# Seven on-chip slots instead of one for the first phase's g blocks

## The chip, the cores and the metric

The kernel runs on one core of a Trainium2 chip. The metric is the device time of one execution in microseconds (us). The kernel before takes 461.11 us, the median of three runs (458.97 to 461.44).

## The reference

Three layers run one after the other on 2304 tokens (4 batches of 576) of width 512. Only what bears on the change is given in full:

```python
def reference(q, k, v, w_in, w_out, phi, w1, w2):
    x = attention(q, k, v)                        # [2304, 512]; local heads and strided heads
    h = x @ w_in                                  # [2304, 2048]
    g = h * (1.0 / (1.0 + np.exp(-1.702 * h)))
    x = g @ w_out                                 # [2304, 512]
    logits = x @ phi                              # [2304, 32]
    d = softmax(logits, axis=0)                   # over tokens
    c = softmax(logits, axis=1)                   # over the 32 slots
    slot_input = d.T @ x                          # 8 experts, 4 slots each
    slot_out = [relu(s @ w1[e]) @ w2[e] for e, s in enumerate(slot_input)]
    return c @ slot_out
```

## The kernel before

**Tiling.** The tokens are cut into six chunks (`LIVE`): four steps of up to 512 tokens, then 256 each. The 2048 columns of g are cut into 16 blocks f of 128. A step is a pair (c, f): chunk c outer, block f inner, 96 steps in all. The first phase is c = 0, the second c = 1, and so on.

**One step** (`moe_step`, L374). `gemm1` (L326) makes h for the step: 12 matmuls of 128x128 by 128x512 into one of two PSUM tiles (`ps_h`, two buffers, L334). Then ScalarE writes tanh(0.851 h) into an SBUF slot (L339) and VectorE turns this in place into (tanh + 1) * h (L340). That is twice g. A slot is a 128x512 piece of the tile `gT` (19 of them), picked by `g_slot` (L310).

**What happens to g.** In c = 0 the logits can't be formed yet, because the second weight matrix is not converted. So each block is written to DRAM (`g_scr`, L398) from the SP queue, and the slot is given back at once in the program's order (L399). From c = 3 on, pieces of it are read back (L324). In c = 1 and later, g stays on chip: VectorE transposes it into the slot numbered f of `gT` (L362), and four blocks at a time go into the logits (`lg`, L354). The first `lg` matmuls come in the middle of c = 1, after the step (1, 4).

**Which slot.** `g_slot` takes the first free one of slots 16 to 18 (with `NF` = 16), then 14 and 15. Since L399 frees the slot in every step of c = 0, all 16 blocks of that phase get slot 16. The tile framework adds the wait that this needs: the tanh of block f+1 may write only when the transfer of block f out of the slot has landed.

**What else runs in these phases.** The weights come as 64-bit numbers (`wraw`) and are converted on chip. `load_w` (L262) needs one ScalarE operation (L268), one on GpSimd (L269) and three on VectorE (L270, L271, L272). For the first weight matrix follow a rounded copy on ScalarE (L279) and the remainder on GpSimd (L280). The raw input of the first matrix lies in slots 0 to 11 of `gT` (L255 to L259), in pairs used in turn by six blocks. In c = 0, the 16 blocks of the first matrix are converted two to three steps ahead, and then the second matrix's, which are written to `wo_scr` (L284), transposed (L287) and multiplied by phi (L297, L303). Between these steps a generator runs the attention of the next batch: scores `s` (L167), mask, maximum and exp (L170, L180, L185), normalising on GpSimd (L188), transposes `ptp` (L203), products `av` (L222) and copies into x (L247, L248).

**What sets the order.** Each engine executes its own queue in order, and so does SP with its DMAs. The order in these queues is not that of the source: a scheduler in the tile framework orders the instructions by its own estimates of when each could start, and the slot of g is one of the things that it sees.

Of the kernel before, what the change touches and what calls it, by code (L numbers as in the profile page):

```python
# [33 lines left out]
NF = FF // 128  # L34
# [10 lines left out]
def tile_kernel(ctx: ExitStack, tc: tile.TileContext, lqk, lv, sqk, sv, wraw, phi, wexp, cst, out):  # L45
# [207 lines left out]
    def load_raw(f, k):  # L253
        if gt and k == 0:
            r = 2 * (f % 6)  # L255
            raw = gt[0][:, r:r + 2].rearrange("p a b -> p (a b)").bitcast(U32).rearrange("p (a b) -> p a b", b=2)
        else:
            raw = rawp.tile([P, 512, 2], U32, tag="raw", name=f"raw_{f}_{k}")
        nc.sync.dma_start(raw.rearrange("p a b -> p (a b)"), wraw[f, k].bitcast(U32))  # L259
        raws[f, k] = raw  # L260

    def load_w(f, k):  # L262
        if (f, k) not in raws:
            load_raw(f, k)
        raw = raws.pop((f, k))
        t = rawp.tile([P, 512], F32, tag="wc", name=f"wc_{f}_{k}", bufs=4)
        u = t.bitcast(U32)
        nc.scalar.activation(t, raw[:, :, 1].bitcast(F32), AF.Abs)  # L268
        nc.gpsimd.tensor_scalar(t, t, F64_LARGE, F64_SMALL, op0=ALU.min, op1=ALU.max)  # L269
        nc.vector.tensor_scalar(u, u, 3, 0x3FFFFFF8, op0=ALU.logical_shift_left, op1=ALU.bitwise_and)  # L270
        nc.vector.scalar_tensor_tensor(u, raw[:, :, 1], 0xC0000000, u, op0=ALU.bitwise_and, op1=ALU.bitwise_or)  # L271
        nc.vector.scalar_tensor_tensor(u, raw[:, :, 0], 29, u, op0=ALU.logical_shift_right, op1=ALU.bitwise_or)  # L272
        conv[f, k] = t

    def split(f):
        if f % 2 == 0:
            wis[f // 2] = wip.tile([P, 2, 2, 512], F32R, tag="wi", name=f"wi_{f // 2}")
        w, t = wis[f // 2][:, f % 2], conv.pop((f, 0))
        nc.scalar.copy(w[:, 0], t)  # L279
        nc.gpsimd.tensor_tensor(w[:, 1], t, w[:, 0].bitcast(F32), op=ALU.subtract)  # L280

    def wo_transpose(f):
        t = conv.pop((f, 1))
        nc.sync.dma_start(wo_scr[f], t)  # L284
        tp = mtile(f"wot_{f}")
        for kt in range(4):
            nc.tensor.transpose(tp[:, 128 * kt:128 * kt + 128], t[:, 128 * kt:128 * kt + 128], ident)  # L287
        woT[f] = rawp.tile([P, 4, 128], F32, tag="woT", name=f"woT_{f}", bufs=1)
        nc.scalar.copy(woT[f].rearrange("p k f -> p (k f)"), tp)
# [3 lines left out]
    def wo_phi(f):  # L293
        t = woT.pop(f)
        pw = mtile(f"wp_{f}")[:, :P]
        for kt in range(4):
            nc.tensor.matmul(pw[32 * kt:32 * kt + 32], phs[:, kt, :], t[:, kt, :], start=True, stop=True)  # L297
        wpT[f] = rawp.tile([P, P], F32, tag="wpT", name=f"wpT_{f}", bufs=2)
        nc.scalar.mul(wpT[f], pw, 0.5)

    def wo_phi_sum(f):
        pw = mtile(f"wq_{f}")[:, :NS]
        nc.tensor.matmul(pw, wpT.pop(f), sel, start=True, stop=True)  # L303
        nc.scalar.copy(wp[:, f, :], pw)
# [3 lines left out]
    slots, taken, where = {}, set(), {}  # L308

    def g_slot(c, f):  # L310
        k = next(k for k in [*range(NF, NF + 6), NF - 2, NF - 1] if k in slots and k not in taken)
        assert k >= NF or c < 2
        taken.add(k)
        where[c, f] = k
        return slots[k]
# [5 lines left out]
    def g_open(c, f):  # L321
        g = gs[c, f] = g_slot(c, f)
        if c in KEPT:
            nc.scalar.dma_start(g[:, :256], g_scr[f, :, KEPT[c]:KEPT[c] + 256])  # L324

    def gemm1(c, f):  # L326
        c0, N = LIVE[c]
        x, w = xt[c0 // 512], wis[f // 2][:, f % 2]
        xs = slice(c0 % 512, c0 % 512 + N)
        h = ps_h.tile([P, 512], F32, tag="h", name=f"h_{c}_{f}")  # L330
        n = 0
        for kt in range(4):
            for we, xe in ((0, 0), (0, 1), (1, 0)):
                nc.tensor.matmul(h[:, :N], w[:, we, 128 * kt:128 * kt + 128], x[xe][:, kt, xs], start=n == 0, stop=n == 11)  # L334
                n += 1
        if (c, f) not in gs:
            g_open(c, f)
        g = gs[c, f][:, 256:] if c in KEPT else gs[c, f][:, :N]
        nc.scalar.activation(g, h[:, :N], AF.Tanh, scale=0.851)  # L339
        nc.vector.scalar_tensor_tensor(g, g, 1.0, h[:, :N], op0=ALU.add, op1=ALU.mult)  # L340
# [8 lines left out]
    def logits(c, f0):  # L349
        N = WIDTH[c]  # L350
        if f0 == 0:
            lgs[c] = ps_lg.tile([P, 512], F32, tag="lg", name=f"lg_{c}")
        for j in range(4):
            nc.tensor.matmul(lgs[c][32 * j:32 * j + 32, :N], wp[:, f0 + j, :], gs[c, f0 + j][:, :N], start=f0 == 0, stop=f0 == NF - 4)  # L354
            g_used(c, f0 + j)

    def g_transpose(c, f):
        N = WIDTH[c]
        if c < 5:
            assert f not in taken  # L360
            taken.add(f)
        nc.vector.transpose(t_slots(c)[:, f, :N], gs[c, f][:, :N])  # L362
        g_used(c, f)
# [4 lines left out]
    def moe_step(i):  # L368
        c, f = steps[i]
        j = i - NF  # L370
        for n in (i + 4, i + 5):
            if n < NF and (n, 0) not in raws and n not in done_in:
                load_raw(n, 0)
        if i + 3 < NF:  # L374
            done_in.add(i + 3)
            load_w(i + 3, 0)
        if 0 <= j + 3 < NF:
            load_w(j + 3, 1)
        if 0 <= j < NF:
            wo_phi(j)  # L380
        if 0 < j < NF:
            wo_phi_sum(j - 1)
        for s in list(side):
            if next(s, True):
                side.remove(s)
        if i + 2 < NF:
            split(i + 2)
        if c == 1 or f >= TFROM:
            for _ in range(1 if c == 1 else 2):
                if todo and (c > 1 or todo[0][1] not in taken):  # L390
                    g_transpose(*todo.pop(0))
        while todo and todo[0][0] < c and todo[0][1] not in taken:
            g_transpose(*todo.pop(0))
        gemm1(c, f)
        if 0 <= j + 1 < NF:
            wo_transpose(j + 1)
        if c == 0:
            nc.sync.dma_start(g_scr[f], gs[c, f])  # L398
            taken.discard(where.pop((c, f)))  # L399
            return  # L400
        if j and f % 4 == 0:
            pc, pf = steps[i - 4]
            logits(pc, pf)
            if f == 0:
                side.append(post(pc))
        todo.append((c, f))
        if f + 1 < NF and c in KEPT:
            g_open(c, f + 1)
# [172 lines left out]
    for i, (c, f) in enumerate(steps):  # L581
        if f == 0 and c < 3:
            side.append(attention_steps(c + 1))
            next(side[-1])
        if (c, f) == (2, 0):
            wo_phi_sum(NF - 1)
            raw_es.close()
            accp = acc_es.enter_context(tc.tile_pool(name="accp", bufs=1))
            sp_["p"] = accp
            acc = accp.tile([P, 4, 512], F32, name="acc")  # L590
            more = accp.tile([P, 3, 512], F32, name="more")
            slots.update({NF + 3 + k: more[:, k] for k in range(3)})
        if (c, f) == (3, 2):
            att_es.close()
            e1p = ctx.enter_context(tc.tile_pool(name="e1p", bufs=4, side="right"))
            for _ in range(4):
                load_ex(e1p, "e")
            for e in (1, 0, 1):
                load_ex(xp, f"x{e}")
        if (c, f) == (5, 1):  # L600
            for e in range(2):
                load_ex(xp, f"x{e}")
        moe_step(i)
        if (c, f) == (5, 4):
            for k in range(2):
                load_ex(None, gx_tile())
        if c == 5 and f % 2:
            load_ex(wip, "wi")
# [4 lines left out]
    c = len(LIVE) - 1  # L613
# [231 lines left out]
```

## Time and profile before

| | |
|---|---|
| median of three runs | 461.11 us |
| the profiled execution | 463.21 us |
| its span in the trace | 461.1 us |
| TensorE (PE) busy | 418.4 us, 91% |
| VectorE (DVE) busy | 272.1 us, 59% |
| ScalarE (ACT) busy | 197.2 us, 43% |
| GpSimd (POOL) busy | 77.8 us, 17% |
| DRAM written | 13.11 MB |

The span goes from the first instruction to the last; 2.1 us of the profiled execution lie outside it. These shares are means over stages that have different limits, so the sections below look at stretches of the span. Times in the trace are us from its start. A TensorE block `h` is 12 matmuls. Busy PE means that a matmul is under way, whatever the clock that was granted to it; that clock is given as a fraction of full speed.

### The profile page before, as it was taken

To read this page: it belongs to the slowest core of one execution; us is meant where nothing else is said; L and a number is where in the kernel's file an instruction comes from. 1 tells how busy PE (TensorE), PEld (TensorE's weight loads), DVE (VectorE), ACT (ScalarE), POOL (GpSimd) and SP (SyncE) were. 2 spreads that over 40 slices of the span, in tenths; PEclk is the share of its full clock that TensorE was granted. 3 is DMA by queue.
4 is the path that set the end of the run, shared out by engine and by line. 5 is a ranking of instruction groups with operands and counts; after the bars stand their busy time and mean duration, and the time that the engine had idled before them with its cause. 6 is when DMAs were issued, how large, how long until landed. Compare 5 with 4: busy or idle time off the path is not lost.

```text
span 461.1 us, 10584 instructions
## 1 busy us (share of the span) xinstructions
PE 418.4 (91%) x4272; PEld 302.4 (66%) x4277; DVE 272.1 (59%) x580; ACT 197.2 (43%) x656; POOL 77.8 (17%) x96
## 2 busy tenths in 40 slices
PE   8969859578979999999999999999999999799964
PEld 4746647456757777777767767778778797244654
DVE  2784999992737667755564565477486464432212
ACT  3876567653645566755634353212212222120311
POOL 0461658830121111100210010000000000010000
PEclk9999978799989999999999999999999999899985
DMA  8966766267643747125020016922122998879996
GB/s 234 374 180 248 217 218 230 73 209 267 173 148 92 230 136 221 72 91 179 18 93 22 16 42 215 383 69 70 48 59 70 353 354 316 342 280 427 422 347 208
DMA packets 32528, 89.32 MB, mean 194 GB/s; under 512 B 2912, under 2 KB 14304, under 8 KB 28384
## 3 DMA queue, kind: packets, MB, share of 16 engines
q1 hardware_dynamic: 27872, 84.45, 52.7%
q10 hardware_dynamic: 4608, 4.20, 3.0%
q8 instruction: 34, 0.56, 0.5%
q14 instruction: 14, 0.11, 0.1%
HBM read 75.53 MB, written 13.11 MB: 192 GB/s over the span
## 4 chain that ended last, share of the span: by engine, by line
PE 67%; DVE 16%; DMA 7%; ACT 4%; issue 2%; POOL 2%; SPq 0%; ACTq 0%; POOLq 0%
PE h L334 37%; PE u L462 4%; PE lg L354 4%; DMA out<-gT 4%; DVE wc L271 4%; PE s L167 4%; DVE wc L272 3%; PE hp L677 3%; PE av L222 2%; PE op L707 2%; PE ptp L203 2%; DVE wc L270 2%; ACT ts L185 2%; DMA qk<-lqk 2%; PE wot L287 1%
## 5 line engine op out<-in xcount | busy, mean ns | idle before, releaser
L334 PE MATMUL h<-x,wi 128*128 128x512 f32 (+1 forms) x1152 | 231.1, 353 | 15.7 <-DVE gT L340 15.3
L334 PEld LDWEIGHTS h<-x,wi 128*128 128x128 f32 x1152 | 179.7, 195 | 57.9 <-issue 17.2
L340 DVE SCALAR_TENSOR_TENSOR gT<-gT,h 128x512 f32<-128x512 f32 (+1 forms) x78 | 44.3, 568 | 66.0 <-ACT gT L339 65.2
L339 ACT ACTIVATE gT<-h 128x512 f32<-128x512 f32 (+1 forms) x78 | 39.1, 501 | 76.0 <-PE h L334 65.2
L185 ACT ACTIVATE ts<-ts,nmx 128x64 f32<-128x64 f32 (+1 forms) x120 | 41.6, 350 | 27.0 <-DVE nmx L180 27.0
L188 POOL TENSOR_TENSOR ts<-ts,sm 128x384 f32<-128x384 f32 (+2 forms) x32 | 28.6, 894 | 132.5 <-DVE sm L187 75.1
L362 DVE STREAM_TRANSPOSE gT<-gT 128x512 f32<-128x512 f32 (+1 forms) x62 | 40.0, 651 | 3.1 <-DMA gT<-g_scr 1.6
L269 POOL TENSOR_SCALAR wc<-wc 128x512 f32<-128x512 f32 x32 | 23.5, 739 | 51.7 <-ACT wc L268 48.6
L203 PE MATMUL ptp<-cs,ts 128*96 128x128 f32 (+1 forms) x120 | 18.7, 290 | 10.0 <-POOL ts L188 8.5
L167 PE MATMUL s<-qk 64*64 64x96 f32 (+1 forms) x552 | 26.3, 236 | 0.3 <-DMA qk<-lqk 0.3
L167 PEld LDWEIGHTS s<-qk 64*64 64x64 f32 x552 | 21.5, 134 | 6.4 <-issue 4.5
L270 DVE TENSOR_SCALAR wc<-wc 128x512 uint32<-128x512 uint32 x32 | 19.4, 617 | 10.4 <-POOL wc L269 8.5
L280 POOL TENSOR_TENSOR wi<-wc,wi 128x512 fp32r<-128x512 f32 x16 | 22.9, 1439 | 8.7 <-ACT wi L279 6.4
L203 PEld LDWEIGHTS ptp<-cs,ts 128*96 128x96 f32 (+1 forms) x120 | 13.8, 141 | 16.0 <-POOL ts L188 13.8
L735 POOL MEMSET hz<- 128x512 f32 x4 | 2.1, 560 | 126.9 <-PE spp L630 126.9
L248 DVE TENSOR_TENSOR x<-av,x 128x320 fp32r<-128x320 f32 (+20 forms) x54 | 19.5, 393 | 6.0 <-ACT x L247 5.6
L185 ACT ACTIVATION_READ_ACCUMULATOR ts<-ts,nmx 128x1 f32 x120 | 22.8, 190 | 0.0
L247 ACT CAST x<-av 128x320 fp32r<-128x320 f32 (+20 forms) x54 | 19.0, 397 | 8.8 <-PE av L222 4.6
L462 PE MATMUL u<-gT,dT 32*32 32x512 f32 x576 | 20.9, 615 | 1.9 <-DVE z L437 1.9
L339 ACT ACTIVATE more<-h 128x256 f32<-128x256 f32 (+1 forms) x18 | 7.7, 427 | 34.5 <-PE h L334 28.1
L186 DVE TENSOR_SCALAR sm<-sm 128x5 f32<-128x5 f32 (+2 forms) x32 | 7.9, 247 | 22.7 <-ACT ts L185 22.7
L354 PE MATMUL lg<-gT,wp 128*32 128x512 f32 (+1 forms) x124 | 21.1, 563 | 0.0
(127 smaller groups left out, 509.7 us busy)
## 6 DMA issues: line engine op xcount, KB each, us to landing
ex<-wexp SPq DMA_DIRECT2D x28, 1024.0 KB, 8.2
raw<-wraw SPq DMA_DIRECT2D x19, 512.0 KB, 4.8
gT<-wraw SPq DMA_DIRECT2D x13, 512.0 KB, 4.4
qk<-lqk SPq DMA_DIRECT2D x8, 592.0 KB, 5.8
g_scr<-gT SPq DMA_DIRECT2D x16, 256.0 KB, 3.0
wo_scr<-wc SPq DMA_DIRECT2D x16, 256.0 KB, 2.3
ex<-wo_scr SPq DMA_DIRECT2D x4, 1024.0 KB, 9.2
gT<-wexp SPq DMA_DIRECT2D x4, 1024.0 KB, 7.0
```

Source lines behind the costliest of these rows:

```text
L167: nc.tensor.matmul(sp[hs, u], t[hs, qo:qo + 64], t[hs, ko + qo:ko + qo + nk], start=not early, stop=not early or u == nt - 1)
L185: nc.scalar.activation(ts[:, u], src[:, u], AF.Exp, scale=sc, bias=nmx[:, u:u + 1], accum_out=sm[:, u:u + 1])
L188: nc.gpsimd.tensor_tensor(ts, ts, sm[:, :nt].unsqueeze(2).to_broadcast([P, nt, nk]), op=ALU.mult)
L203: nc.tensor.transpose(ptp[:nk, u - a], src, ident)
L269: nc.gpsimd.tensor_scalar(t, t, F64_LARGE, F64_SMALL, op0=ALU.min, op1=ALU.max)
L270: nc.vector.tensor_scalar(u, u, 3, 0x3FFFFFF8, op0=ALU.logical_shift_left, op1=ALU.bitwise_and)
L334: nc.tensor.matmul(h[:, :N], w[:, we, 128 * kt:128 * kt + 128], x[xe][:, kt, xs], start=n == 0, stop=n == 11)
L339: nc.scalar.activation(g, h[:, :N], AF.Tanh, scale=0.851)
L340: nc.vector.scalar_tensor_tensor(g, g, 1.0, h[:, :N], op0=ALU.add, op1=ALU.mult)
L354: nc.tensor.matmul(lgs[c][32 * j:32 * j + 32, :N], wp[:, f0 + j, :], gs[c, f0 + j][:, :N], start=f0 == 0, stop=f0 == NF - 4)
L362: nc.vector.transpose(t_slots(c)[:, f, :N], gs[c, f][:, :N])
L462: nc.tensor.matmul(us[a][32 * j:32 * j + 32, :].rearrange("p (t f) -> p t f", f=32), dT[q, 32 * b:32 * b + 32], gT[q, :, 32 * b:32 * b + 3 ...
```

## The change

In c = 0, block f takes slot 12 + f % 7, so that slots 12 to 18 are used in turn. None of them is one of the slots 0 to 11 that hold raw weights in that phase. The bookkeeping of free slots is then not needed for c = 0. The arithmetic, the number of instructions on each engine and the bytes moved stay as they were.

```diff
@@ -308,8 +308,10 @@
     slots, taken, where = {}, set(), {}
 
     def g_slot(c, f):
+        if c == 0:
+            return slots[NF - 4 + f % 7]
         k = next(k for k in [*range(NF, NF + 6), NF - 2, NF - 1] if k in slots and k not in taken)
-        assert k >= NF or c < 2
+        assert k >= NF or c == 1
         taken.add(k)
         where[c, f] = k
         return slots[k]
@@ -396,7 +398,6 @@
             wo_transpose(j + 1)
         if c == 0:
             nc.sync.dma_start(g_scr[f], gs[c, f])
-            taken.discard(where.pop((c, f)))
             return
```

The scheduler orders the queues anew. Two places show it. In the changed kernel the lines below the edit have numbers that are 2 higher, and L398 becomes L400.

The first place is VectorE's queue around the conversion of block 3 of the second weight matrix (`wc_3_1`), with the last scores of the first attention batch beside it. `h_0_8` is the h of c = 0, f = 8; before:

```order
L270 TENSOR_SCALAR wc_3_1_1411<-wc_3_1_1411 128x512
L271 SCALAR_TENSOR_TENSOR wc_3_1_1411<-raw_3_1_1409,wc_3_1_1411 128x512
L340 SCALAR_TENSOR_TENSOR gT_587<-gT_587,h_0_8_1041 128x512
L170 SCALAR_TENSOR_TENSOR ts_1_3_1104<-s_1_3_1_1213,maskb_100 128x5x64
L272 SCALAR_TENSOR_TENSOR wc_3_1_1411<-raw_3_1_1409,wc_3_1_1411 128x512
L180 TENSOR_REDUCE nmx_1_3_1_1225<-ts_1_3_1104 128x5
L186 TENSOR_SCALAR sm_1_3_1_1227<-sm_1_3_1_1227 128x5
L187 RECIPROCAL sm_1_3_1_1227<-sm_1_3_1_1227 128x5
L340 SCALAR_TENSOR_TENSOR gT_587<-gT_587,h_0_9_1079 128x512
L340 SCALAR_TENSOR_TENSOR gT_587<-gT_587,h_0_10_1135 128x512
L340 SCALAR_TENSOR_TENSOR gT_587<-gT_587,h_0_11_1191 128x512
```

and in the changed kernel:

```order
L186 TENSOR_SCALAR sm_1_3_1_1227<-sm_1_3_1_1227 128x5
L187 RECIPROCAL sm_1_3_1_1227<-sm_1_3_1_1227 128x5
L342 SCALAR_TENSOR_TENSOR gT_587<-gT_587,h_0_13_1278 128x512
L270 TENSOR_SCALAR wc_3_1_1411<-wc_3_1_1411 128x512
L271 SCALAR_TENSOR_TENSOR wc_3_1_1411<-raw_3_1_1409,wc_3_1_1411 128x512
L272 SCALAR_TENSOR_TENSOR wc_3_1_1411<-raw_3_1_1409,wc_3_1_1411 128x512
L248 TENSOR_TENSOR x1_1_311<-av_1_3_1_1303,x0_1_310 128x14x14
L248 TENSOR_TENSOR x1_1_311<-av_1_3_0_1302,x0_1_310 128x18x14
L248 TENSOR_TENSOR x1_2_791<-av_1_3_1_1303,x0_2_790 128x14x4
L248 TENSOR_TENSOR x1_2_791<-av_1_3_0_1302,x0_2_790 128x18x4
L342 SCALAR_TENSOR_TENSOR gT_587<-gT_587,h_0_14_1334 128x512
L342 SCALAR_TENSOR_TENSOR gT_587<-gT_587,h_0_15_1358 128x512
```

At that conversion the queue has finished block 8 before and block 13 in the changed kernel, and all 16 blocks stand right behind it. The orders of the engines run together again at about the step (1, 6); the first `lg` matmuls come at the same place in both.

The second place is SP's queue from the first write of g on; before:

```order
L259 DMA gT_587<-wraw 128x1024 x5
L398 DMA g_scr_85<-gT_587 128x512
L259 DMA gT_587<-wraw 128x1024 x3
L398 DMA g_scr_85<-gT_587 128x512
L120 DMA v_1_1_865<-lv 96x1152
L259 DMA gT_587<-wraw 128x1024
L110 DMA qk_1_2_908<-sqk 128x1208
L398 DMA g_scr_85<-gT_587 128x512
L259 DMA gT_587<-wraw 128x1024 x3
L398 DMA g_scr_85<-gT_587 128x512
L259 DMA gT_587<-wraw 128x1024
```

and in the changed kernel:

```order
L259 DMA gT_587<-wraw 128x1024 x5
L400 DMA g_scr_85<-gT_587 128x512
L259 DMA gT_587<-wraw 128x1024 x2
L400 DMA g_scr_85<-gT_587 128x512
L259 DMA gT_587<-wraw 128x1024
L120 DMA v_1_1_865<-lv 96x1152
L400 DMA g_scr_85<-gT_587 128x512
L259 DMA gT_587<-wraw 128x1024
L110 DMA qk_1_2_908<-sqk 128x1208
L400 DMA g_scr_85<-gT_587 128x512
L259 DMA gT_587<-wraw 128x1024
L400 DMA g_scr_85<-gT_587 128x512
```

The eight raw loads behind the first write of g (f = 8 to 15) now have seven such writes between them, where four stood before.

## Rows read from the trace of the kernel before

**Rows 1.** Stretches: bounds, length, then busy PE, PEld, DVE, ACT, POOL (instructions), PEclk, DMA share, GB/s.
```profile
44.66:157.72 113.06, 90.92 (x734) 69.91 (x734) 86.45 (x149) 62.28 (x193) 46.42 (x48) 0.91 0.58 184
52.00:105.00 53.00, 37.35 (x289) 28.66 (x290) 52.60 (x86) 32.29 (x99) 35.08 (x32) 0.84 0.60 196
105.00:139.40 34.40, 29.32 (x221) 22.36 (x221) 14.89 (x31) 16.49 (x55) 4.47 (x7) 0.95 0.58 183
139.40:153.80 14.40, 13.32 (x118) 10.34 (x116) 9.22 (x18) 7.14 (x24) 1.57 (x2) 1.00 0.53 153
157.72:220.00 62.28, 62.28 (x599) 45.21 (x599) 38.91 (x81) 39.09 (x138) 8.78 (x14) 1.00 0.45 149
220.00:461.00 241.00, 227.34 (x2481) 162.61 (x2480) 120.98 (x279) 68.88 (x204) 8.62 (x14) 0.96 0.54 198
```

**Rows 2.** Waits from 42 to 140 us: who waited for whom, total us, times, longest.
```profile
PE h L334 <- DVE gT L340: 14.2, 7, 4.8
DVE gT L340 <- ACT gT L339: 13.9, 5, 5.7
ACT gT L339 <- DMA g_scr<-gT: 10.7, 6, 2.7
```

**Rows 3.** DMA issues: operation, queue, count, KB each, median us to landing.
```profile
raw<-wraw SPq DMA_DIRECT2D x19, 512.0 KB, 4.8
g_scr<-gT SPq DMA_DIRECT2D x16, 256.0 KB, 3.0
```

**Rows 4.** The chain that ended last, 103 to 159 us: start, us, what (count).
```profile
103.62 3.53 DMA g_scr<-gT
...
108.58 3.09 DMA g_scr<-gT
...
117.11 0.64 PE s L167 x10
...
121.34 0.36 PE wp L297 x8
121.69 0.81 PE s L167 x16
...
133.42 0.34 PE ptp L203 x3
...
139.19 1.00 PE s L167 x20
...
147.94 0.34 PE wq L303 x2
148.28 1.20 PE av L222 x36
149.47 2.96 PE h L334 x12
152.44 0.44 PE wot L287 x4
...
157.79 1.00 PE lg L354 x8
```

**Rows 5.** DVE timeline: start, us, operation, form, count, [idle before, releaser].
```profile
102.91 0.68 DVE L340 SCALAR_TENSOR_TENSOR gT<-gT,h 128x512 f32<-128x512 f32 x1
...
104.51 0.48 DVE L180 TENSOR_REDUCE nmx<-ts 128x5 f32<-128x320 f32 x1
...
107.03 0.19 DVE L187 RECIPROCAL sm<-sm 128x5 f32<-128x5 f32 x1
...
117.44 1.65 DVE L248 TENSOR_TENSOR x<-av,x 128x252 fp32r<-128x252 f32 x4 [0.73 <-ACT x L247]
...
138.71 0.68 DVE L340 SCALAR_TENSOR_TENSOR gT<-gT,h 128x512 f32<-128x512 f32 x1
```

**Rows 6.** PE timeline, same columns.
```profile
85.93 5.49 PE L334 MATMUL h<-x,wi 128*128 128x512 f32 x12 [4.78 <-DVE gT L340]
...
128.45 0.55 PE L203 MATMUL ptp<-cs,ts 128*96 128x128 f32 x3 [1.94 <-POOL ts L188]
```

## The prediction

> **What bounds the kernel now.** I read the stretches first, then the waits, then the chain and the timelines of VectorE (DVE) and TensorE (PE) in the first two phases.
>
> The stretches [rows 1] show where time can be won at all. From 157.72 to 220 us PE is busy for 62.28 of 62.28 us at full clock, and after 220 for 227 of 241 us. Nothing of the change is there, and the expert weights that are loaded late go into buffers that this same work empties. So a microsecond won before 157.7 us should reach the end whole, and one that is not won there is not won. The reader should see three different stages ahead of that point. From 52 to 105 us DVE is busy for 52.60 of 53.00 us: it converts weights, and PE has only 37.35 us of matmuls. From 105 to 139.4 us neither is full: DVE 14.89 and PE 29.32 of 34.40 us. From 139.4 us on PE is nearly full (13.32 of 14.40 us).
>
> The waits [rows 2] name the link of the middle stage. ScalarE's tanh waits 10.7 us in six pieces for the write of g to leave the only slot; DVE's second step waits 13.9 us for that tanh; PE waits 14.2 us for DVE to empty the h tile. The chain [rows 4] runs over these writes, 3.53 and 3.09 us from issue to landing, like the median of 3.0 us [rows 3]. The waits understate it: where the scheduler put the tanh of a block late in ScalarE's queue, because it counts on the transfer, other instructions fill the wait, but the block is late all the same. The block that begins at 85.93 us does so after 4.78 us without work, and takes 5.49 us where an undisturbed one takes 2.96 [rows 6, 4]. The clock is the reason: the mean granted clock in this stage is 0.84 and not 1.00 [rows 1], so part of it runs at 1.2 and not 2.4 GHz, after PE has stood idle.
>
> **The change, part by part.** The numbers of instructions, their sizes, the bytes and the issues on SP are the same: no term for them. The bookkeeping is done when the program is built and costs nothing. The write of a block must now land before the block seven later, and not the next one: with the blocks of the changed kernel no closer than 2.96 us, seven take over 20 us against 3.0 for the landing. I cost this wait at nothing; its cover is six blocks of matmuls. The rest is how far the blocks of the first phase move forward, in three steps.
>
> *1. When the first phase ends.* In the new DVE order all 16 blocks are through right after the last scores of the first attention batch. Before, DVE is done with those scores' maximum at 105.0 us (104.51 + 0.48), with no idle time worth naming since 52 us, and has then finished nine blocks [rows 5]. In the changed queue up to block 15 stand, beyond that work, seven more block steps, two small ones of 0.2 us (before at 107 us), and four copies into x that before come at 117.44 us in 1.65 us. A block step takes 0.60 us of the queue (102.91 to the next at 103.51). That makes 7 x 0.60 + 0.4 + 1.65 = 6.2 us, so a DVE that stays full ends block 15 at 111.2 us. Before it ended at 139.4 us. PE is done with this block before the tanh and the DVE step, 1.3 us earlier: 109.9 us.
>
> *2. What PE still has to do until the first logits* (157.8 us before). The new PE order between block 15 and the first `lg` holds five blocks at 2.96, six weight transposes at 0.44, five products with phi at 0.36, four sums at 0.34, scores of 0.64, 0.81, 1.00 and again 0.81, nine transposes of probabilities in 0.55 + 0.34, and one batch of values at 1.20 [rows 4, 6]: 14.8 + 2.6 + 1.8 + 1.4 + 3.3 + 0.9 + 1.2 = 26.0 us. From 109.9 us, with no gap, the logits begin at 135.9 us: 21.9 us earlier. That is the upper end.
>
> *3. What gets lost on the way.* From 44.66 to 157.72 us PE is busy for 90.92 us [rows 1]. Less the 26.0, 64.9 us stand before 109.9 us, in a room of 65.2. At the clock that it had, PE would thus be as full as DVE; at full clock it has some room, since blocks of 5.49 us then take 2.96. Two full engines that wait for each other in fixed orders lose something. No row shows them both full. The nearest is the stretch from 139.4 us, without any wait for a write: PE idles there for 1.08 of 14.40 us, 7.5%. The worst is the middle stage, 5.08 of 34.40 us, 15%. On 65 us this makes 4.9 us (bounds 0 and 10). On the 26.0 us it makes 2.0, and I add one wait of the transposes for the softmax of their own batch, 1.94 us [rows 6], as the scores now stand closer to them: 3.9 (bounds 0 and 6). I take 7.5% because the slot no longer makes anyone wait.
>
> **The sum:** 21.9 - 4.9 - 3.9 = 13.1 us, with ends at 6 and 22. Against the profiled execution, 463.2 us, this gives 450.1; the median of the runs lies 2.1 us below that execution, so **448 us**. The bounds alone give 439 to 455. Next in line, when the write is no longer late: PE waiting for the DVE step of the block two before, in a stage that DVE fills.
>
> **The rivals.**
> *A. DVE keeps the stage (chance 0.17).* From 52 to 105 us DVE has 0.4 us free, and the change takes no work off it. If the added steps do not find their tanh ready, conversions and blocks stay at the pace of now until 105 us, and the change only closes the gaps behind: 5.08 us of PE idle time from 105 to 139.4 us, and 1.7 us from the clock there (0.95 on average: a tenth of 34.4 us at half speed). That is 6.8 us, 454 us. For it speaks a DVE that is full; against it, that PE has 15 us idle in this stage and that the blocks cost DVE only 0.60 us each. The Trainium skill has this case as a rule (Perfetto Trace Analysis, Identifying the Most-Contended Engine): improve the engine with the highest occupancy first, and by it the stage up to 105 us would gain nothing. My step 1 goes past it by one thing: it lets DVE's stage get 6 us longer and takes the work out of the stage behind.
>
> *B. The SP queue turns it round (slower, chance 0.07).* The eight raw loads of blocks 8 to 15 stand behind seven writes of g where they stood behind four, and a write holds the queue until its DVE step is done. A raw load takes 4.8 us to land (another load of the same size, [rows 3]). If four of the eight come too late by that whole time, conversions lose 19.2 us, 6 more than the forecast's gain: 467 us. It decides from three loads on (14.4 us). Against it: a load waits anyway for the conversion six blocks earlier, which frees its pair of slots, so it has the time of six conversions. By 105 us 16 blocks of the first matrix and 4 of the second are converted, fewer than 20 of them in the 53 us of the stage: over 2.6 us each, some 16 us for six.
>
> *C. No change (0.09).* The tanh waits for something else that is as late as the write: the split weights, or x. Then the 10.7 us return under another name, within 2.3 us of 461.1. Against it: behind 105 us DVE and PE both have time to spare and the raw weights of the first matrix are long converted.
>
> **How the numbers follow.** The forecast has 0.65, and 0.02 is left for more than 22 us. A measurement of this kernel can tell about 0.5%, 2.3 us, from no change. Faster by more: 0.65 + 0.02 + 0.17 = 0.84; within it: 0.09; slower: 0.07. The range goes from 441 us, a gain of 20 with little lost, to 457 us, which takes in A with some 3 us on top. It leaves out B and C, the very top of step 2 and the tail.
>
> **What would show it.** Right: no wait of a tanh for a write of g; the last block step of the first phase between 111 and 120 us; the first logits between 140 and 150 us instead of 157.8; DVE still full until some 110 us; the granted clock from 52 to 105 us above 0.84; the distance from the first logits to the end the same as now within 2 us (303.3 us). For A: the last block step only after 125 us, and conversions no later than now. For B: DVE waits for ScalarE's and GpSimd's conversion steps, and these for raw loads, between 60 and 100 us. I would be wrong on the mechanism if the first logits came 13 us earlier and the end did not: then something behind, such as the late weight loads, sets the end by itself.

## The result and the profile after

The changed kernel takes 443.79 us (median of 4 runs, 442.54 to 445.47) against 461.27 us for the kernel before in the same session (4 runs): a ratio of 0.9635 with a 95% interval of 0.959 to 0.9679. It is faster. The profiled execution took 444.09 us with a span of 442.0 us, 19.1 us less in both than the one of before. The execution that was profiled before took 1.9 us more than the median of its runs, the one after 0.3 us more, so the traces show 1.6 us more of a gain than the 17.5 us of the medians. In the changed file the tanh stands in L341, VectorE's second step in L342, the first matrix product in L336, the logits in L356.

The stretches of the changed kernel, with the columns of [rows 1]; the first two have the bounds of before, the others go from the first logits on:

```profile
52.00:105.00 53.00, 43.42 (x332) 32.71 (x330) 48.11 (x88) 35.47 (x113) 33.05 (x31) 0.94 0.59 196
105.00:120.00 15.00, 14.43 (x143) 11.54 (x143) 9.88 (x22) 9.07 (x32) 2.88 (x4) 1.00 0.93 320
120.00:138.92 18.92, 18.92 (x180) 14.39 (x178) 15.18 (x30) 11.78 (x37) 4.55 (x7) 1.00 0.56 170
138.92:202.00 63.08, 63.08 (x603) 45.58 (x603) 40.06 (x84) 40.25 (x142) 9.23 (x14) 1.00 0.48 157
202.00:442.00 240.00, 226.81 (x2478) 162.01 (x2477) 120.24 (x276) 68.12 (x202) 8.12 (x13) 0.97 0.54 199
```

From 52 to 105 us PE does 43.42 us of matmuls where it did 37.35, at a clock of 0.94 and not 0.84 of full speed. VectorE does more block steps in this stretch and is yet *less* busy, 48.11 instead of 52.60 us; this is the row that the prediction did not foresee. Behind the first logits nothing has changed: PE is full, and later as busy as in the last row of [rows 1].

The waits from 42 to 140 us, as in [rows 2]:

```profile
ACT gT L341 <- PE h L336: 12.0, 8, 2.8
...
DVE gT L342 <- ACT gT L341: 8.1, 9, 2.4
PE ptp L203 <- POOL ts L188: 6.6, 4, 2.5
...
PE h L336 <- DVE gT L342: 3.5, 4, 1.4
```

Three DMA issues, as in [rows 3]; `gT<-wraw` are the raw loads into slots 0 to 11, those of blocks 8 to 15 among them:

```profile
raw<-wraw SPq DMA_DIRECT2D x19, 512.0 KB, 4.7
gT<-wraw SPq DMA_DIRECT2D x13, 512.0 KB, 4.3
...
g_scr<-gT SPq DMA_DIRECT2D x16, 256.0 KB, 2.5
```

The writes land half a microsecond sooner, the raw weights as before. The tanh waits for PE and no longer for a write, and PE waits for VectorE's step for 3.5 us where it waited for 14.2. Two blocks' steps on VectorE, the tenth block (number 9) and the last one (15), and PE's work around block 15 and at the first logits (columns as in [rows 5, 6]):

```profile
87.03 0.69 DVE L342 SCALAR_TENSOR_TENSOR gT<-gT,h 128x512 f32<-128x512 f32 x1
...
113.48 0.69 DVE L342 SCALAR_TENSOR_TENSOR gT<-gT,h 128x512 f32<-128x512 f32 x1 [2.04 <-ACT gT L341]
```

```profile
107.74 5.07 PE L336 MATMUL h<-x,wi 128*128 128x512 f32 x21
112.65 0.60 PE L287 MATMUL wot<-cs,wc 128*128 128x128 f32 x4
...
138.94 1.07 PE L356 MATMUL lg<-gT,wp 128*32 128x512 f32 x8
```

PE is through with block 15 at 112.65 us and begins the logits at 138.94, 18.85 us earlier than in [rows 4]. From there to the end of the span it is 303.1 us, as before (303.3). So all of the gain lies ahead of the first logits. Where it lies there is read from one stretch, from 44.66 us (the start of [rows 1]'s first row) to the first logits, in which PE does nearly the same work in every kernel (717 to 738 records of matmuls in those quoted): first the kernel before, then the changed one.

```profile
44.66:157.79 113.13, 90.99 (x738) 69.98 (x742) 86.45 (x149) 62.35 (x194) 46.42 (x48) 0.91 0.58 184
```

```profile
44.66:138.94 94.28, 84.13 (x734) 64.50 (x732) 79.64 (x147) 61.41 (x189) 45.86 (x48) 0.96 0.65 212
```

PE's idle time is the length less its busy time: 22.1 us before, 10.2 after. That is 12.0 us; the other 6.9 us are PE's own work, which takes 84.13 instead of 90.99 us, at a mean granted clock of 0.96 instead of 0.91. In that stretch the trace has the clock at the lower of its two levels (1.2 GHz) for 20.5 us before, 18.0 of them with PE busy, and for 6.8 us after, all of them with PE busy. Half of the busy time at that level is 9.0 and 3.4 us, so by this estimate the clock makes 5.6 of the 6.9 us. I use this stretch as the yardstick for the experiments too.

### The profile page after: what moved, and what is told of

Same layout as the page of the kernel before. It is cut to its first block, busy times and chain, and to the rows that moved or that the text cites. A ratio compares the mean times of both kernels' runs of the same rounds, so it can differ in the third digit from the quotient of the medians.

```text
span 442.0 us, 10589 instructions
## 1 busy us (share of the span) xinstructions
PE 411.7 (93%) x4272; PEld 296.8 (67%) x4277; DVE 266.4 (60%) x580; ACT 196.9 (45%) x656; POOL 77.2 (17%) x96
## 4 chain that ended last, share of the span: by engine, by line
PE 74%; DVE 9%; DMA 7%; ACT 4%; POOL 4%; issue 1%; SPq 0%; ACTq 0%; POOLq 0%; DVEq 0%
PE h L336 39%; PE u L463 5%; PE s L167 5%; PE lg L356 4%; DMA out<-gT 4%; PE hp L678 3%; PE av L222 3%; PE ptp L203 3%; PE op L708 2%; ACT ts L185 2%; DVE wc L271 2%; POOL ts L188 2%; PE wot L287 2%; DVE wc L272 1%; DVE wc L270 1%
## 5 line engine op out<-in xcount | busy, mean ns | idle before, releaser
L336 PE MATMUL h<-x,wi 128*128 128x512 f32 (+1 forms) x1152 | 226.4, 347 | 5.0 <-DVE gT L342 4.6
L336 PEld LDWEIGHTS h<-x,wi 128*128 128x128 f32 x1152 | 175.2, 191 | 45.7 <-issue 17.2
L342 DVE SCALAR_TENSOR_TENSOR gT<-gT,h 128x512 f32<-128x512 f32 (+1 forms) x78 | 44.4, 569 | 55.1 <-ACT gT L341 54.1
L341 ACT ACTIVATE gT<-h 128x512 f32<-128x512 f32 (+1 forms) x78 | 39.1, 501 | 73.4 <-PE h L336 73.1
L188 POOL TENSOR_TENSOR ts<-ts,sm 128x384 f32<-128x384 f32 (+2 forms) x32 | 28.6, 895 | 137.3 <-DVE sm L187 70.9
L269 POOL TENSOR_SCALAR wc<-wc 128x512 f32<-128x512 f32 x32 | 23.3, 735 | 27.2 <-ACT wc L268 24.3
L167 PE MATMUL s<-qk 64*64 64x96 f32 (+1 forms) x552 | 25.4, 236 | 0.0
L280 POOL TENSOR_TENSOR wi<-wc,wi 128x512 fp32r<-128x512 f32 x16 | 22.6, 1413 | 11.0 <-ACT wi L279 11.0
L341 ACT ACTIVATE more<-h 128x256 f32<-128x256 f32 (+1 forms) x18 | 7.7, 427 | 35.8 <-PE h L336 32.7
L270 DVE TENSOR_SCALAR wc<-wc 128x512 uint32<-128x512 uint32 x32 | 17.3, 551 | 10.4 <-POOL wc L269 10.4
L356 PE MATMUL lg<-gT,wp 128*32 128x512 f32 (+1 forms) x124 | 21.1, 563 | 0.0
L186 DVE TENSOR_SCALAR sm<-sm 128x5 f32<-128x5 f32 (+2 forms) x32 | 5.9, 186 | 21.5 <-ACT ts L185 21.5
```

What stands on the lines that cost most here:

```text
L167: nc.tensor.matmul(sp[hs, u], t[hs, qo:qo + 64], t[hs, ko + qo:ko + qo + nk], start=not early, stop=not early or u == nt - 1)
L188: nc.gpsimd.tensor_tensor(ts, ts, sm[:, :nt].unsqueeze(2).to_broadcast([P, nt, nk]), op=ALU.mult)
```

## The experiments

The theory behind the prediction was that the one slot delays the blocks, by its wait at run time and by the places that the scheduler gives the tanh, and that with more slots the blocks move forward. What it did not say is which of the two matters, and whether seven slots are needed. The rivals were that VectorE keeps the stage (A), that other waits take the place of the write (C), and that the blocks behind the middle stage alone bring the gain.

### Seven slots, but every queue in the order of before; and one slot in the order of the changed kernel

Both kernels get a table of instruction numbers for each engine and an ordering between neighbours on one engine, which costs no instruction and no wait:

```diff
         tile_kernel(tc, **args)
+        keep_order(nc, tc)
...
+        for p, q in zip(names, names[1:]):
+            tc.add_manual_dep(by_name[q], p, edge, reason="order")
```

> Seven slots, but every engine and SP keeps the queue order that the scheduler gave the kernel before. My theory (the slot costs mostly through where the blocks stand in the queues): only the waits of the tanh for the write vanish, blocks stay late in VectorE's queue, and the gain is at most the 6.8 us of rival A: 454 to 459 us, with nine blocks done at 105 us. Rival (the waits at run time are what costs, the new order is a by-product): as the changed kernel, 442 to 446 us.

Measured: 459.71 us, ratio 0.9972 (0.9943 to 1.0001): no change that can be told. The traces of both kernels show that the orders were held: until 15 us behind the first logits, VectorE, ScalarE and GpSimd run the same operations on the same tiles in the same order as in the kernel whose order was taken (239, 352 and 75 instructions). The stretch 52 to 105 us of the first kernel, nearly the same as before, and the waits from 42 to 140 us:

```profile
52.00:105.00 53.00, 37.07 (x289) 28.01 (x285) 50.89 (x84) 32.39 (x99) 34.85 (x33) 0.84 0.57 188
```

```profile
PE h L336 <- DVE gT L342: 11.5, 6, 4.7
...
DVE gT L342 <- ACT gT L341: 10.6, 3, 6.5
```

No tanh waits for a write in this kernel. And still VectorE waits for the tanh for 10.6 us and PE for VectorE for 11.5, because the tanh stands in ScalarE's queue behind other work. The block steps come as late as before (block 15 at 139.60 us). To take the wait away alone is worth nothing: this is rival C's picture, waits that return under other names, but only as long as the order stays.

> One slot, but every engine and SP has the queue order of the changed kernel. My theory: the early blocks now wait at run time for the write of the block before, about 2.5 to 3 us each, and ScalarE's queue holds the conversions behind them; part of the gain stays, 448 to 458 us. Rival (waits are all): as the kernel before, 459 to 463 us, or slower. Rival (order is all): as the changed kernel, 442 to 446 us.

Measured: 451.1 us, ratio 0.9774 (0.9722 to 0.9825), some 10 us faster. Its stretch 52 to 105 us and the wait for the write:

```profile
52.00:105.00 53.00, 41.03 (x344) 30.86 (x339) 43.69 (x82) 32.59 (x101) 33.68 (x32) 0.97 0.56 190
```

```profile
ACT gT L339 <- DMA g_scr<-gT: 11.9, 4, 3.3
```

The new order with the old slot gives 10 us, although the tanh now waits 11.9 us for writes. In the yardstick PE's work takes 83.80 us here, as in the changed kernel, and its idle time is 16.0 us (99.78 to the first logits, less 83.80). So the order brings 7 us of PE's work, with the clock at its lower level for 3.4 us and not 20.5, and 6 us of idle time (13 us against the profiled execution of before, 10 us by the medians); the missing wait brings 6 us of idle time more, but only in this order. The run-time wait is the smaller part of the price of one buffer. The larger one is an order that a scheduler wrote because it counted on the wait.

### Three slots and two slots

```diff
-            return slots[NF - 4 + f % 7]
+            return slots[NF + f % 3]
```

> Three slots in turn (16 to 18) instead of seven; the queue orders come out the same as in the changed kernel, so only the run-time wait can differ. A write that lands 2.5 us after its issue is over long before the block three later (at least 3 x 2.96 us): 442 to 446 us, and no wait of a tanh for a write. A theory by which all seven are needed gives 446 us or more.

Measured: 443.99 us, ratio 0.9626 (0.9568 to 0.9684). In its trace VectorE, ScalarE and GpSimd have exactly the order of the changed kernel.

> Two slots in turn; queue orders almost as in the changed kernel. Two blocks later is at least 5.9 us after, against tanh 0.6 + last step 0.6 + write 2.5 to 3 plus the SP queue: little or no wait, 442 to 447 us. If the SP queue often holds the writes back, waits of a tanh for a write come back and it takes 447 to 453 us.

With `f % 2` it is 441.78 us, ratio 0.9585 (0.9526 to 0.9644), with no wait of a tanh for a write. Both intervals overlap that of seven slots. A second slot gives the whole gain: a write lands in 2.5 us (median in the changed kernel), and two blocks that follow each other give it at least the time of one whole block, 2.96 us on PE [rows 4].

### Seven slots for half of the blocks

```diff
-            return slots[NF - 4 + f % 7]
+            return slots[NF - 4 + f % 7 if f >= 9 else NF]
```

> One slot for the blocks f < 9 and seven for the rest. My theory (the gain comes from blocks that move into the stage that VectorE fills): up to 105 us nothing changes, then seven blocks of 2.96 us and the attention's work follow with little waiting; the gain is what rival A gave, about 5 to 9 us: 452 to 456 us. If the waits of the middle stage were the whole matter: 442 to 446 us.

> Seven slots for the blocks f < 9, one for the rest. My theory: nine blocks done by about 87 us as in the changed kernel, then six that wait for the write before them; with the one-slot pace of about 4 us the first phase ends near 119 us instead of 114, and the gain is 10 to 14 us: 447 to 451 us. If only the middle stage counts: 455 to 461 us.

Measured: seven slots from block 9 on give 452.67 us, ratio 0.9794 (0.9746 to 0.9843); seven slots up to block 8 (`f < 9`) give 445.99 us, ratio 0.9652 (0.9612 to 0.9692). The stretch 52 to 105 us of the first of them, and the one behind it:

```profile
52.00:105.00 53.00, 36.70 (x288) 28.05 (x289) 52.72 (x86) 33.01 (x100) 35.08 (x32) 0.87 0.59 196
105.00:122.00 17.00, 17.00 (x119) 13.87 (x118) 5.98 (x13) 7.04 (x21) 0.72 (x1) 1.00 0.76 237
```

With the slots only behind block 8, the first stage stays as it was: VectorE busy for 52.72 of 53 us. The gain is some 9 us, two more than rival A allowed (6.8 us), and it comes by A's mechanism: from 105 us to the end of block 15 PE has no gap and the full clock. But the early half alone gives some 16 of the 17 us, a little more than I had expected of it. So A holds for the middle stage, and is refuted for the first one: blocks do move forward into a stage in which VectorE is shown as full. The two halves make 25 us together, not 17; they win the same time in part.

### The write without the slot

```diff
-        nc.sync.dma_start(g_scr[f], gs[c, f])
+        nc.sync.dma_start(g_scr[f], xt[0][0][:, 0].bitcast(F32))
```

> The kernel before with one slot, but each of the 16 writes takes its 256 KB from x instead of from the slot, so the slot is held by the block's own two steps only; what lands in DRAM is not g, so the later chunks get other numbers. My theory (it is the transfer that holds the slot): nearly the changed kernel, 443 to 448 us, with the tanh waiting at most for VectorE's step of the block before. If one slot as such were the matter: above 452 us.

Measured: 442.08 us, ratio 0.9572 (0.9535 to 0.9609), block 15's step at 113.35 us, the first logits at 138.81 us: the changed kernel, with one slot. The later chunks compute with wrong numbers here; the work is the same. The scheduler, too, gives this kernel the order of the changed one, but for a few neighbours in each queue. What had to go is that a transfer holds the slot that the next tanh writes. The number of slots, the place in memory and the traffic play no part. In this kernel SP's queue does not wait for VectorE's block step either. The changed kernel keeps these waits, 23.6 us of them from 42 to 140 us, and is as fast, so they are not what had to go.

### What VectorE's busy time holds

The puzzle that was left is VectorE: 4.5 us less busy from 52 to 105 us, where 11 block steps begin instead of 8, and 41 conversion steps (L270 to L272) instead of 44. VectorE and GpSimd (POOL) side by side in the changed kernel's timeline, first VectorE, then GpSimd:

```profile
51.86 0.41 DVE L270 TENSOR_SCALAR wc<-wc 128x512 uint32<-128x512 uint32 x1
...
52.36 0.68 DVE L271 SCALAR_TENSOR_TENSOR wc<-gT,wc 128x512 uint32<-128x512 uint32 x1
...
53.43 1.32 DVE L272 SCALAR_TENSOR_TENSOR wc<-gT,wc 128x512 uint32<-128x512 uint32 x1
...
55.83 1.51 DVE L270 TENSOR_SCALAR wc<-wc 128x512 uint32<-128x512 uint32 x1
...
58.62 0.65 DVE L272 SCALAR_TENSOR_TENSOR wc<-gT,wc 128x512 uint32<-128x512 uint32 x1
```

```profile
52.68 1.52 POOL L280 TENSOR_TENSOR wi<-wc,wi 128x512 fp32r<-128x512 f32 x1 [1.20 <-ACT wi L279]
54.17 1.62 POOL L269 TENSOR_SCALAR wc<-wc 128x512 f32<-128x512 f32 x2
55.77 1.28 POOL L280 TENSOR_TENSOR wi<-wc,wi 128x512 fp32r<-128x512 f32 x1
58.85 1.27 POOL L188 TENSOR_TENSOR ts<-ts,sm 128x480 f32<-128x480 f32 x1 [1.80 <-DVE sm L187]
```

The same operation L270 takes 0.41 us at 51.86 and 1.51 us at 55.83. The second began 0.06 us after GpSimd's L280, which ended at 57.05; L270 ended at 57.34, 0.29 us later. L272 at 53.43 began within GpSimd's L280, which ended at 54.20, and took until 54.75, 0.55 us later; at 58.62 it began before GpSimd's L188 and took 0.65. That looks like VectorE standing still until GpSimd's instruction is over. Even a step on 128x4 elements shows it, in the kernel before, VectorE first and GpSimd second:

```profile
60.70 0.15 DVE L186 TENSOR_SCALAR sm<-sm 128x5 f32<-128x5 f32 x1
...
66.38 1.24 DVE L186 TENSOR_SCALAR sm<-sm 128x4 f32<-128x4 f32 x1
```

```profile
66.00 1.59 POOL L280 TENSOR_TENSOR wi<-wc,wi 128x512 fp32r<-128x512 f32 x1 [0.76 <-ACT wi L279]
```

The traces of all thirteen kernels, from 44.6 us to the first logits, leave no exception. A step with two operands in SBUF (L271, L272 and, on VectorE, L280) that began while GpSimd was at work ended 0.51 to 0.64 us after GpSimd's instruction, whatever was left of it (225 steps); the 390 others took 0.64 to 0.69 us. L270 ended 0.28 to 0.37 us after it (104 steps); the 200 others took 0.38 to 0.48 us. By the undisturbed durations (0.68, 0.42 and 0.16 us for L186) VectorE stood still inside its instructions for 15.1 us from 52 to 105 us before, and for 9.9 us after; that is the 4.5 us and more. The test moves one GpSimd operation, the remainder of the split weights (L280), to VectorE, which the trace shows as the fuller engine:

```diff
-        nc.gpsimd.tensor_tensor(w[:, 1], t, w[:, 0].bitcast(F32), op=ALU.subtract)
+        nc.vector.tensor_tensor(w[:, 1], t, w[:, 0].bitcast(F32), op=ALU.subtract)
```

> The changed kernel with the remainder of the first weight matrix (16 operations, L280) on VectorE instead of GpSimd. It tells what fills VectorE there: if its conversion steps take 0.9 to 1.1 us instead of 0.6 to 0.7 because GpSimd works at the same time, they fall to about 0.7 us, VectorE's busy time grows by less than the 16 x 0.6 us, and the kernel takes 440 to 446 us. If the long steps have another cause, VectorE's stage grows by 9.6 us and the kernel takes 448 us or more.

Measured: **432.7 us**, ratio 0.9357 (0.9314 to 0.9399), 11 us faster than the changed kernel and more than I had expected. The groups of VectorE's conversion from 44.6 to 105 us (busy, mean ns of one | idle before), first in the changed kernel, then with the remainder on VectorE:

```profile
L272 DVE SCALAR_TENSOR_TENSOR wc<-gT,wc 128x512 uint32<-128x512 uint32 x13 | 14.7, 1136 | 0.0
L271 DVE SCALAR_TENSOR_TENSOR wc<-gT,wc 128x512 uint32<-128x512 uint32 x13 | 11.5, 886 | 0.0
L270 DVE TENSOR_SCALAR wc<-wc 128x512 uint32<-128x512 uint32 x16 | 9.5, 614 | 0.8 <-POOL wc L269 0.8
L342 DVE SCALAR_TENSOR_TENSOR gT<-gT,h 128x512 f32<-128x512 f32 x13 | 8.8, 679 | 3.7 <-ACT gT L341 3.5
```

```profile
L280 DVE TENSOR_TENSOR wi<-wc,wi 128x512 fp32r<-128x512 f32 x13 | 11.1, 855 | 0.0
L342 DVE SCALAR_TENSOR_TENSOR gT<-gT,h 128x512 f32<-128x512 f32 x15 | 10.1, 674 | 1.0 <-ACT gT L341 1.0
L271 DVE SCALAR_TENSOR_TENSOR wc<-gT,wc 128x512 uint32<-128x512 uint32 x13 | 9.9, 759 | 0.0
L272 DVE SCALAR_TENSOR_TENSOR wc<-gT,wc 128x512 uint32<-128x512 uint32 x13 | 9.2, 705 | 0.0
L270 DVE TENSOR_SCALAR wc<-wc 128x512 uint32<-128x512 uint32 x17 | 8.1, 479 | 1.6 <-POOL wc L269 1.6
```

VectorE has 11.1 us of new work, and its three conversion steps fall from 35.7 to 27.2 us in sum (14.7 + 11.5 + 9.5 against 9.9 + 9.2 + 8.1), with one conversion step more among them. In the yardstick PE's idle time falls to 5.1 us and its work to 79.19 us (17 records fewer than in the changed kernel), at a clock of 1.00:

```profile
44.66:128.95 84.29, 79.19 (x717) 59.99 (x716) 79.15 (x160) 59.51 (x186) 26.99 (x33) 1.00 0.73 241
```

But the edit also saves a change of engine on the way of the weights, and the scheduler orders the queues anew for it, so a second test gives GpSimd work that no one needs, in the place of the one taken away, and leaves VectorE's and ScalarE's queues in the order of the first test:

```diff
+        j = rawp.tile([P, 256], F32, tag="idle", name=f"idle_{f}", bufs=1)
+        for i in (0, 256):
+            nc.gpsimd.tensor_tensor(j, w[:, 0, i:i + 256].bitcast(F32), w[:, 0, i:i + 256].bitcast(F32), op=ALU.subtract)
```

> The kernel with the remainder on VectorE, and on GpSimd, at the place in its queue where the remainder stood, two subtractions of 128x256 a block into a tile that nobody reads. All queues keep their order; no step waits for the added work but GpSimd's own next one. If VectorE is slower while GpSimd works, its conversion steps of 0.71 and 0.76 us go back towards 0.9 to 1.1 us and most of the 11 us is lost: 440 to 448 us. If moving the remainder helped by saving a change of engine on the way to the matmuls, nothing that waits has changed: within 2 us of 432.7, the steps as short as there.

Measured: 440.71 us, ratio 0.9544 (0.9506 to 0.9581). The same groups:

```profile
L280 DVE TENSOR_TENSOR wi<-wc,wi 128x512 fp32r<-128x512 f32 x13 | 12.6, 969 | 0.0
L271 DVE SCALAR_TENSOR_TENSOR wc<-gT,wc 128x512 uint32<-128x512 uint32 x13 | 11.1, 852 | 0.0
L272 DVE SCALAR_TENSOR_TENSOR wc<-gT,wc 128x512 uint32<-128x512 uint32 x13 | 10.1, 778 | 0.0
...
L270 DVE TENSOR_SCALAR wc<-wc 128x512 uint32<-128x512 uint32 x16 | 8.6, 540 | 1.6 <-POOL wc L269 1.6
```

Work whose result no one needs costs 8.0 of the 11 us. All four kinds of step are longer, by 61 to 114 ns each, 4.4 us for 13 of each. The steps do not go back all the way (L272 stays at 0.78 and not 1.14 us), so the size rests on which instructions happen to meet. By the undisturbed durations VectorE stood still for 11.2 us in the yardstick, against 5.9 in the first test: 5.3 us more. A part of the 8.0 us may come another way: GpSimd's own later work stands behind the added one, and PE's wait for its normalising (L188) grows from 2.9 to 4.8 us. What is left, 3 us, can be the saved change of engine or the new order; that I did not separate.

> Seven slots, the remainder and the clamp of the raw weights both on VectorE, so that GpSimd keeps only its work on probabilities in the first stages. VectorE gets some 30 clamps of 0.3 to 0.6 us more, 9 to 18 us over 150 us. If what remains of the long VectorE steps (0.70 to 0.76 us with the remainder moved) is still due to GpSimd's clamps, they fall to about 0.6 us and the time stays within 2 us of 432.7 or falls. If VectorE's own work now bounds the stage, the time rises by up to 10 us, to 435 to 443 us.

With the clamp (L269) on VectorE as well (`nc.vector.tensor_scalar` for `nc.gpsimd.tensor_scalar`): 435.56 us, ratio 0.9427 (0.9393 to 0.9461), 2.9 us more than with the remainder alone (the two intervals just overlap), at the lower end of what I had named for a stage bound by VectorE's own work. L272 stays at 0.72 us, L271 falls to 0.71 and L270 to 0.45, but 14 clamps of 0.41 us come on top. With GpSimd almost out of the way, nothing more was won.

> The kernel before, with its one slot, and only the remainder of the split weights on VectorE instead of GpSimd. If the two engines side by side are a cost of their own, added to that of the one slot, the 11.1 us that this edit gave on top of seven slots come here too, about 450 us. If the waits for the write set the blocks' pace behind some 60 us whatever VectorE does, quicker conversions are of little use: 455 to 461 us, with the tanh waiting for writes in sum at least the 10.7 us of before. If the edit alone gives more than half of 28 us (under 447 us), the one slot was no bound of its own.

The kernel before with only the remainder on VectorE: 444.76 us, ratio 0.9623 (0.9587 to 0.9659). That is under the 447 us at which I meant to call the one slot no bound of its own, and that reading would have been wrong: seven slots take the same kernel from 444.8 to 432.7 us. The tanh still waits for writes here:

```profile
ACT gT L339 <- DMA g_scr<-gT: 7.4, 8, 1.9
```

Two costs lie side by side, each worth some 17 us when it goes first and 11 to 12 us when it goes second.

## Why the prediction was right, and where it was off

The forecast was 448 us, faster; the result is 443.8 us, in the range. Against the profiled execution the sum forecast 13.1 us, and 19.1 were won, 17.5 by the medians.

*Step 1, the first phase's end: the time nearly right, the reason wrong.* Forecast for a full VectorE: block 15 through at 111.2 us, PE done with it at 109.9. Found: the step begins at 113.48 us and is through at 114.17, and PE is done at 112.65. But VectorE was not full until then, 48.11 of 53 us, and its last step waited 2.04 us for the tanh. I added the new steps to an engine at 52.60 of 53 us and took each busy microsecond for work. A good part was waiting for GpSimd, as the groups of the kernel before show for 44.6 to 105 us:

```profile
L272 DVE SCALAR_TENSOR_TENSOR wc<-gT,wc 128x512 uint32<-128x512 uint32 x13 | 14.6, 1132 | 0.0
L271 DVE SCALAR_TENSOR_TENSOR wc<-gT,wc 128x512 uint32<-128x512 uint32 x13 | 13.1, 1015 | 0.0
L270 DVE TENSOR_SCALAR wc<-wc 128x512 uint32<-128x512 uint32 x17 | 11.3, 686 | 1.2 <-POOL wc L269 1.2
```

By the undisturbed 0.68 and 0.41 us of the rows above, these steps held 14.9 us of waiting before (an estimate) and 11.9 us after. That the time came out near with this engine misread is luck.

*Step 2, PE's work to the logits: right.* 26.0 us forecast, 26.3 found (112.65 to 138.94), with PE busy all the time. One term was read wrongly without harm: the nine transposes were priced by two rows of three each, at 0.89 us, and take 0.92 (121.40 to 122.32).

*Step 3, the losses: the step that failed.* I took 4.9 us on the work up to block 15 and 3.9 us behind it. Found are 2.8 (112.65 less 109.9) and 0.3. The 5.7 us between 8.8 and 3.1 are what was missing from the sum; by the medians it is 1.6 us less, the difference of the two profiled executions from their medians. PE up to its end of block 15 and from there to the first logits, in the changed kernel:

```profile
44.66:112.65 67.99, 57.84 (x485) 44.17 (x484) 59.33 (x105) 43.95 (x130) 39.71 (x39) 0.95 0.64 212
112.65:138.94 26.29, 26.29 (x250) 20.33 (x248) 20.31 (x42) 17.47 (x59) 6.16 (x9) 1.00 0.66 214
```

The reason is a term that I named and then costed at nothing: the clock. I let PE's 90.92 us of [rows 1] stand as they were and put losses on top. PE did idle for 10.2 us, more than the 4.9 that I took in that part, but its work there was 57.84 us and not the 64.9 of the sum: its longest wait for VectorE fell from 4.8 to 1.4 us, and the granted clock rose from 0.91 to 0.96 over the stretch. Behind block 15, where I had added 2.0 us of idle time and a wait of 1.94 us, PE had other products in its queue and no gap at all. My bounds reached down to no loss, so the result lies in the range.

*The wait for the write, costed at nothing: right*, with room to spare, as two slots show. *That the distance from the first logits to the end stays: right* (303.1 against 303.3 us), and 300.2 to 304.9 us in the eleven experiments.

*That the late tanh is a matter of the queue's order*, which stood in the reading of the waits, is shown now: without the order the change gives nothing, without the slots the order gives 10 us.

*The rivals.* A, VectorE keeps the stage, is refuted for seven slots and found, with 9 and not 6.8 us, in the kernel whose slots come only from block 9 on. The rule of the Trainium skill that I set beside it (Perfetto Trace Analysis, Identifying the Most-Contended Engine: the engine with the highest occupancy first, and for VectorE occupancy as a fair measure) takes VectorE's 52.60 of 53 us for a measure of its work. This trace does not agree: the stage got shorter with VectorE's work unchanged, and shorter again with 11.1 us *added* to it. B, the SP queue, did not happen: the raw loads into slots 0 to 11 land in 4.3 us (4.4 before), and no engine waits for one in the view of the waits, although SP's queue waits 23.6 us for block steps before it writes g. C came only where the order was held.

*The signs named ahead.* No wait for a write, block 15 between 111 and 120 us, the clock over 0.84 and the distance to the end came out as named. The first logits came at 138.9 instead of 140 to 150 us, for step 3's reason; a VectorE full until 110 us did not come, for step 1's.

## What to carry to other kernels

A buffer that a transfer holds costs more than the wait in the trace where a scheduler sets the order: look how far back it put the next writer, and try a second buffer before many. An engine that is shown as busy all the time may be standing still inside its instructions: compare long and short ones of the same operation and shape, and see what ran beside the long ones, before calling it the bound. Where a change takes idle time from PE in a stage whose granted clock is below 1.00, count the clock as a term of its own.

## What the runs showed of the hardware that I had not expected

VectorE's conversion steps get longer by about what is left of GpSimd's instruction: 0.41 to 1.51 us and 0.65 to 1.32 us for the same operation and size, and 0.15 to 1.24 us for a step on a few elements. The block step L342, which reads h from PSUM and only one operand from SBUF, does not: 679, 674 and 673 ns on average from 44.6 to 105 us in the changed kernel, with the remainder on VectorE and with the idle work on GpSimd; the 91 block steps of the thirteen kernels that began while GpSimd was at work took 0.67 to 0.69 us each. The Trainium skill states such a rule (SBUF — State Buffer, Who interferes with whom): VectorE and GpSimd share a pair of ports, the one that comes second stands still until the instruction of the first is over, and of VectorE's operations those with two inputs in SBUF or in a two-port mode are concerned. These rows agree with it in which operations are hit and in when they end; in which mode L270 and L186 ran the profile does not say.

Moving one operation of 128x512 for each of 16 blocks from the engine that the trace shows as busy for 33 of 53 us to one at 48 (35 and 53 with one slot) made the kernel 11 us faster with seven slots, and 17 us with one.
